# Six VectorE operations instead of eight for each chunk of a float64 to float32 conversion, with the exponent test on ScalarE's absolute value

## The chip, the cores and the metric

The kernel runs on one core of a Trainium2 chip. The metric is the device time of one execution in microseconds; lower is better.

## The reference

Three layers follow each other. Attention takes q, k and v of shape 4 x 8 x 576 x 64, with keys and values averaged over groups of 8 positions. A mixture of 8 experts with matrices of 512 x 1024 and 1024 x 512 works on 2304 tokens, with shares that come from eight rounds of normalising rows and columns. A softplus layer of 512 x 2048 and 2048 x 512 ends the work. The last layer's weights are float64 on the way in, because they are multiplied by a float64 scalar; the kernel gets each number as two 32-bit words.

```python
def _moe_ref(x, w_gate, w1, w2):
    ...
    for e in range(E):
        h = np.maximum(x @ w1[e], 0.0)
        ye = h @ w2[e]
        out += P[:, e:e + 1] * ye
    return out.astype(np.float32)

def _moe2_setup():
    ...
    return {'x': ..., 'w_in': np.random.randn(d_model, d_ff).astype(np.float32) * (1.0 / np.sqrt(d_model)), 'w_out': np.random.randn(d_ff, d_model).astype(np.float32) * (1.0 / np.sqrt(d_ff))}

def _moe2_ref(x, w_in, w_out):
    h = x @ w_in
    g = np.maximum(h, 0.0) + np.log1p(np.exp(-np.abs(h)))
    return (g @ w_out).astype(np.float32)
```

## The kernel before

The 2304 tokens are worked in three parts of 768. Six phases follow each other: the experts for parts 0, 1 and 2, then the softplus layer for parts 1, 2 and 0. Each phase is a row of units, a unit being 256 columns of the hidden layer (32 units for the experts of a part, 8 for the softplus layer). Each unit has a first product (`first`, seven products of half blocks by a fast matrix multiplication scheme, with the sums `u`, `za` and `p` on VectorE) and a second product (`second`, six tiles `py` of 128 tokens, each added into `g` on VectorE). Every operand of TensorE is split into a rounded part (`hi`, written by ScalarE) and a remainder (`lo`, written mostly by GpSimd, L282), and each product is made of three matmuls (L734).

The order of every engine's work is the order in which the program is written. Between the products of `first` and behind the tiles of `second` the main loop calls `hook()`. After the attention and a list of side jobs are done, each hook runs the next step of a generator, `from_float64`, up to its next `yield`. So the conversion of the float64 weights lies between the main operations of the first two expert phases, one VectorE operation per hook. Whatever has not run by the third phase is run there at once.

The conversion has 32 chunks of 128 x 512 numbers. `fetch` (L1163) loads the words of the next chunk into one of two `f64` tiles (shown as `f` in the profile). A chunk then has these steps:

- L1179 and L1181: `da` (in PSUM) gets the exponent and mantissa bits of the upper word shifted by three, and the two sign and top exponent bits
- L1183: `db` gets the 11 exponent bits alone
- L1185: the three top bits of the lower word go into `da`
- L1187: `dt` is `da` as a float, or zero where the exponent is under 897
- L1189: `da` keeps sign and exponent of `dt`
- L1191 and L1193: `dr` is the remaining 29 bits of the lower word, scaled by 2 to the -52 and by `da`
- L1194, on GpSimd: `dt` + `dr`; L1195, on SyncE's queue: the store of `dt` into `v1` or `v2`, and two more hooks' ends

`db` and `dt` have the same tag, `ln`, with two buffers in turn, so every `db` lies in the one and every `dt` in the other. The write of a chunk's `dt` must wait until the store of the chunk before has read its buffer out. `dr` shares the tag `ex`, also with two buffers. GpSimd's queue holds, between these additions, the remainders `w1lo` and `w2lo`, the `sums` of the first weights (L279, L282), and in the second phase the subtractions for `t` that the third phase needs. SyncE's queue issues the stores and the loads of weights (L271, L275, L1163, L345) in the order of the program.

Of the kernel before, what the change touches and what calls it, by code (L numbers as in the profile page):

```python
# [9 lines left out]
F32 = mybir.dt.float32  # L10
F32R = mybir.dt.float32r
U32 = mybir.dt.uint32
AF = mybir.ActivationFunctionType
ALU = mybir.AluOpType
# [5 lines left out]
def attention_moe_softplus_kernel(  # L20
# [12 lines left out]
    nc = tc.nc  # L33
# [10 lines left out]
    P = 128  # L44
# [35 lines left out]
    def bank(name, kind="y", dt=F32):  # L80
        if kind not in banks:
            kind = away[0] or ""
        if kind in halves:
            return banks[kind].tile([P, 2, 512], dt, tag=f"two{kind}", name=name)[:, 0, :]
        return banks[kind].tile([P, 512], dt, tag=f"bank{kind}", name=name)
# [1056 lines left out]
    def widths():  # L1142
        for u in range(NU2):
            o = u * US
            src = w_in[:, 2 * o:2 * (o + US)].rearrange("(c p) (f w) -> p c f w", p=P, w=2)
            for s in range(2):
                yield src[:, 2 * s:2 * s + 2], v1[u][:, 2 * s:2 * s + 2, :]
            src = w_out[o:o + US, :].rearrange("(c p) (d w) -> p c d w", p=P, w=2)
            for s in range(2):
                yield src[:, s:s + 1], v2[u][:, s:s + 1, :]  # L1150

    def from_float64():

        ts, stt = nc.vector.tensor_scalar, nc.vector.scalar_tensor_tensor
        every = list(widths())

        def fetch(i):
            if i < len(every):
                src = every[i][0]
                t = extra["f64"] if i % 2 else tpool.tile([P, 2 * UC * HALF], U32, tag="f64", name="f64", bufs=1)  # L1160
                _, c, f, w = src.shape
                raw_t["f64", i] = t.rearrange("p (c f w) -> p c f w", c=c, w=w)
                nc.sync.dma_start(raw_t["f64", i], src)  # L1163

        fetch(0)
        for _ in range(4):
            yield
        for at, (src, dst) in enumerate(every):
            _, c, f, _ = src.shape
            n = c * f  # L1170
            raw = raw_t.pop(("f64", at))
            fetch(at + 1)
            up = raw[:, :, :, 1].rearrange("p c f -> p (c f)")
            dn = raw[:, :, :, 0].rearrange("p c f -> p (c f)")
            a = bank("da", "c", U32)
            b = tpool.tile([P, n], U32, tag="ln", name="db")
            r = tpool.tile([P, n], U32, tag="ex", name="dr")
            t = tpool.tile([P, n], F32, tag="ln", name="dt")
            ts(a, up, 3, 0x3FFFFFF8, op0=ALU.logical_shift_left, op1=ALU.bitwise_and)  # L1179
            yield  # L1180
            stt(a, up, 0xC0000000, a, op0=ALU.bitwise_and, op1=ALU.bitwise_or)  # L1181
            yield
            ts(b, up, 20, 0x7FF, op0=ALU.logical_shift_right, op1=ALU.bitwise_and)  # L1183
            yield
            stt(a, dn, 29, a, op0=ALU.logical_shift_right, op1=ALU.bitwise_or)  # L1185
            yield
            stt(t, b, 897.0, a.bitcast(F32), op0=ALU.is_ge, op1=ALU.mult)  # L1187
            yield
            ts(a, t.bitcast(U32), 0xFF800000, None, op0=ALU.bitwise_and)  # L1189
            yield  # L1190
            ts(r, dn, 0x1FFFFFFF, None, op0=ALU.bitwise_and)  # L1191
            yield
            stt(r.bitcast(F32), r, 2.0 ** -52, a.bitcast(F32), op0=ALU.mult, op1=ALU.mult)  # L1193
            nc.gpsimd.tensor_tensor(t, t, r.bitcast(F32), op=ALU.add)  # L1194
            nc.sync.dma_start(dst.rearrange("p c f -> p (c f)"), t)  # L1195
            yield
            yield


    conversion = from_float64()  # L1200
    side = []
    slot = [0]
# [176 lines left out]
    tpool = None  # L1379
# [47 lines left out]
    for step, (what, n) in enumerate(todo):  # L1427
# [66 lines left out]
        else:  # L1494
# [53 lines left out]
            if attn[0] is None and "" in banks:  # L1548
                part_banks()
                tpool = pools[0]  # L1550
# [30 lines left out]
```

## Time and profile before

| | us |
|---|---|
| median of 3 runs | 1994.94 |
| lowest and highest | 1991.36 and 1995.46 |
| the profiled execution | 1994.42 |
| its span in the trace | 1992.6 |
| TensorE busy | 1959.6 (98%) |
| VectorE busy | 1423.2 (71%) |
| GpSimd busy | 1387.1 (70%) |
| ScalarE busy | 899.7 (45%) |
| conversion, first to last operation | 362 to 1076 |

The page gives the share of the whole span; an engine can be nearly full in one stretch and half empty in another, so the stretches have to be read by themselves. An idle time in brackets behind an instruction is that of its engine just before it, with what ended it. PE is TensorE, DVE is VectorE, ACT is ScalarE, POOL is GpSimd, SPq is the queue of SyncE.

### The profile page before, as it was taken

The page shows a single profiled execution, that of the slowest core. Times are in us where ns is not written, and L with a number is a line of the kernel's source. Part 1 is how long each engine was busy: PE and PEld are TensorE (multiplying, and loading weights), DVE is VectorE, ACT ScalarE, POOL GpSimd, SP SyncE. Part 2 cuts the span into 40 slices and gives each one's busy share as a digit, 9 for nine tenths or more (in the row PEclk, how much of TensorE's full clock was granted, in tenths as well). Part 3 has the DMA queues.
Part 4 walks back from the last instruction along what each step waited for, and adds up shares of the span by engine and source line. Part 5 has one row for each costly group of instructions (what it writes and reads, how often), then busy time and mean ns, then how long its engine had stood idle before and what let it go on. Part 6 is the DMA issues. An engine that isn't in the chain of part 4 may idle for free. (4 is left out here: it accounts for less than half of the span.)

```text
span 1992.6 us, 29835 instructions
## 1 busy us (share of the span) xinstructions
PE 1959.6 (98%) x10786; PEld 1784.2 (90%) x10786; DVE 1423.2 (71%) x2418; ACT 899.7 (45%) x1710; POOL 1387.1 (70%) x1088
## 2 busy tenths in 40 slices
PE   9899999999999999999999999999999999999999
PEld 7688888899889989889988999999999988888998
DVE  6776576887675898679997667678778657556455
ACT  6545434324434233333333454554455566565543
POOL 6765556766676898856766687788888875656553
PEclk9999999999999999999999999999999999999999
DMA  7342222434344655546565644444545523423421
GB/s 198 106 123 73 67 64 65 158 127 153 136 142 162 226 191 201 183 163 211 174 206 173 213 137 128 150 134 138 175 156 142 173 75 130 152 85 119 150 64 64
DMA packets 183249, 283.43 MB, mean 142 GB/s; under 512 B 31676, under 2 KB 111036, under 8 KB 182844
## 3 DMA queue, kind: packets, MB, share of 16 engines
q1 hardware_dynamic: 173020, 267.75, 42.1%
q10 hardware_dynamic: 10080, 13.77, 1.9%
q8 instruction: 85, 1.39, 0.3%
q14 instruction: 64, 0.52, 0.1%
HBM read 216.23 MB, written 65.24 MB: 141 GB/s over the span
## 5 line engine op out<-in xcount | busy, mean ns | idle before, releaser
L734 PE MATMUL p<-xhi,w1hi 128*128 128x384 f32 x1680 | 570.0, 339 | 11.0 <-DVE p L974 8.7
L734 PE MATMUL p<-xhi,w1lo 128*128 128x384 f32 x1680 | 563.9, 336 | 0.0
L734 PE MATMUL p<-xlo,w1hi 128*128 128x384 f32 x1680 | 563.7, 336 | 0.0
L282 POOL TENSOR_TENSOR w1lo<-w1raw,w1hi 128x512 fp32r<-128x512 f32 x240 | 240.7, 1024 | 361.5 <-ACT w1hi L313 361.5
L734 PE MATMUL py<-w2hi,hhi 128*128 128x512 f32 x1056 | 416.5, 394 | 6.6 <-DVE g L1046 3.3
L734 PE MATMUL py<-w2hi,hlo 128*128 128x512 f32 x1056 | 414.7, 393 | 0.0
L734 PE MATMUL py<-w2lo,hhi 128*128 128x512 f32 x1056 | 414.4, 392 | 0.0
L282 POOL TENSOR_TENSOR w2lo<-w2raw,w2hi 128x1024 fp32r<-128x1024 f32 (+1 forms) x178 | 327.5, 1849 | 61.2 <-ACT w2hi L237 45.4
L734 PEld LDWEIGHTS p<-xhi,w1hi 128*128 128x128 f32 x1680 | 316.2, 188 | 27.7 <-DVE p L974 12.4
L734 PEld LDWEIGHTS p<-xlo,w1hi 128*128 128x128 f32 x1680 | 316.3, 188 | 6.8
L734 PEld LDWEIGHTS p<-xhi,w1lo 128*128 128x128 f32 x1680 | 315.9, 188 | 0.0
L282 POOL TENSOR_TENSOR w1lo<-sums,w1hi 128x1024 fp32r<-128x1024 f32 x120 | 288.8, 2406 | 1.9 <-ACT w1hi L313 1.9
L734 PEld LDWEIGHTS py<-w2hi,hhi 128*128 128x128 f32 x1056 | 198.8, 188 | 51.9 <-DVE g L1046 5.4
L734 PEld LDWEIGHTS py<-w2hi,hlo 128*128 128x128 f32 x1056 | 198.6, 188 | 42.2
L747 ACT ACTIVATE hhi<-p 128x384 fp32r<-128x384 f32 x256 | 121.0, 494 | 255.3 <-PE p L734 222.9
L1061 DVE SCALAR_TENSOR_TENSOR g<-py,prob,g 128x512 f32<-128x512 f32 x282 | 209.6, 745 | 31.1 <-PE py L734 27.4
L734 PEld LDWEIGHTS py<-w2lo,hhi 128*128 128x128 f32 x1056 | 198.7, 188 | 35.7
L978 ACT COPY za<-p 128x384 f32<-128x384 f32 x88 | 42.4, 482 | 329.0 <-PE p L734 325.7
L748 DVE SCALAR_TENSOR_TENSOR hlo<-p,hhi 128x384 fp32r<-128x384 f32 x256 | 140.6, 550 | 21.1 <-ACT hhi L747 21.0
L974 DVE TENSOR_TENSOR za<-p,za 128x384 f32<-128x384 f32 x88 | 48.9, 556 | 123.8 <-PE p L734 123.6
L313 ACT CAST w1hi<-sums 128x1024 fp32r<-128x1024 f32 x120 | 126.2, 1052 | 1.8 <-POOL sums L282 1.8
L734 PE MATMUL py<-hhi,w2lo 128*128 128x384 f32 x360 | 121.7, 338 | 0.9 <-POOL w2lo L282 0.9
(159 smaller groups left out, 3168.3 us busy)
## 6 DMA issues: line engine op xcount, KB each, us to landing
w1raw<-in_moe_w_dram SPq DMA_DIRECT2D x96, 512.0 KB
w2raw<-in_moe_w_dram SPq DMA_DIRECT2D x64, 512.0 KB
sums<-sd SPq DMA_DIRECT2D x48, 512.0 KB
sd<-sums SPq DMA_DIRECT2D x32, 512.0 KB
td<-t SPq DMA_DIRECT2D x64, 256.0 KB
w2raw<-td SPq DMA_DIRECT2D x64, 256.0 KB
xlod<-xl ACTq DMA_DIRECT2D x70, 192.0 KB
xlo<-xlod SPq DMA_DIRECT2D x35, 384.0 KB
```

The costliest lines, as they stand in the source:

```text
L282: nc.gpsimd.tensor_tensor(o, a, b, op=ALU.subtract)
L313: nc.scalar.copy(at(hi), src)
L734: nc.tensor.matmul(ps, lhs[a], rhs[b], start=first and i == 0, stop=last and i == 2, skip_group_check=goes_on,)
L747: nc.scalar.activation(hh, src, AF.Relu)
L748: nc.vector.scalar_tensor_tensor(hl, src, 0.0, hh.bitcast(F32), op0=ALU.max, op1=ALU.subtract)
L974: add = lambda o, x, y: nc.vector.tensor_tensor(o, x, y, op=ALU.add)
L978: nc.scalar.copy(a, ps("a"))
L1061: nc.vector.scalar_tensor_tensor(a, py, prob[:, t, e:e + 1], a, op0=ALU.mult, op1=ALU.add)
```

## The change

The exponent test no longer takes the 11 exponent bits out of the upper word. ScalarE writes the absolute value of the upper word, read as a float32, into `db`; its upper exponent bits and the lower three in the mantissa make the comparison with 1.125 x 2 to the -15 the same test as an exponent of at least 897. The three top bits of the lower word are no longer put into `da`; instead the whole lower word, shifted by one, goes into the remainder `dr`. Six VectorE operations and one ScalarE operation are left for a chunk, and seven hooks instead of nine.

```diff
@@ -1173,25 +1173,22 @@
             up = raw[:, :, :, 1].rearrange("p c f -> p (c f)")
             dn = raw[:, :, :, 0].rearrange("p c f -> p (c f)")
             a = bank("da", "c", U32)
-            b = tpool.tile([P, n], U32, tag="ln", name="db")
-            r = tpool.tile([P, n], U32, tag="ex", name="dr")
+            b = tpool.tile([P, n], F32, tag="ln", name="db")
+            r = tpool.tile([P, n], F32, tag="ex", name="dr")
             t = tpool.tile([P, n], F32, tag="ln", name="dt")
             ts(a, up, 3, 0x3FFFFFF8, op0=ALU.logical_shift_left, op1=ALU.bitwise_and)
+            nc.scalar.activation(b, up.bitcast(F32), AF.Abs)
             yield
             stt(a, up, 0xC0000000, a, op0=ALU.bitwise_and, op1=ALU.bitwise_or)
             yield
-            ts(b, up, 20, 0x7FF, op0=ALU.logical_shift_right, op1=ALU.bitwise_and)
-            yield
-            stt(a, dn, 29, a, op0=ALU.logical_shift_right, op1=ALU.bitwise_or)
-            yield
-            stt(t, b, 897.0, a.bitcast(F32), op0=ALU.is_ge, op1=ALU.mult)
+            stt(t, b, 1.125 * 2.0 ** -15, a.bitcast(F32), op0=ALU.is_ge, op1=ALU.mult)
             yield
             ts(a, t.bitcast(U32), 0xFF800000, None, op0=ALU.bitwise_and)
             yield
-            ts(r, dn, 0x1FFFFFFF, None, op0=ALU.bitwise_and)
+            ts(r.bitcast(U32), dn, 1, None, op0=ALU.logical_shift_right)
             yield
-            stt(r.bitcast(F32), r, 2.0 ** -52, a.bitcast(F32), op0=ALU.mult, op1=ALU.mult)
-            nc.gpsimd.tensor_tensor(t, t, r.bitcast(F32), op=ALU.add)
+            stt(r, r.bitcast(U32), 2.0 ** -51, a.bitcast(F32), op0=ALU.mult, op1=ALU.mult)
+            nc.gpsimd.tensor_tensor(t, t, r, op=ALU.add)
             nc.sync.dma_start(dst.rearrange("p c f -> p (c f)"), t)
             yield
             yield
```

In the changed program `dt` is written by line 1184, `dr` by 1188 and 1190, and GpSimd's addition is line 1191; the work of the other lines is the same. The number behind a tile's name tells one buffer's use from another. On VectorE, in a unit of the second phase, from the accumulation before the first product to the sums behind its fourth, before:

```order
L1061 SCALAR_TENSOR_TENSOR g3_3007<-py_7089,prob_88,g3_3007 128x512
L1181 SCALAR_TENSOR_TENSOR da_7084<-f64_3020,da_7084 128x512
L1061 SCALAR_TENSOR_TENSOR g3_3007<-py_7098,prob_88,g3_3007 128x512
L1183 TENSOR_SCALAR db_7085<-f64_3020 128x512
L974 TENSOR_TENSOR u1_7117<-p6_7127,za_7116 128x384
L1185 SCALAR_TENSOR_TENSOR da_7084<-f64_3020,da_7084 128x512
L1187 SCALAR_TENSOR_TENSOR dt_7087<-db_7085,da_7084 128x512
L1189 TENSOR_SCALAR da_7084<-dt_7087 128x512
L974 TENSOR_TENSOR za_7116<-p6_7127,za_7116 128x384
```

and at the same main operations now:

```order
L1061 SCALAR_TENSOR_TENSOR g3_3007<-py_7114,prob_88,g3_3007 128x512
L1190 SCALAR_TENSOR_TENSOR dr_7036<-dr_7036,da_7034 128x512
L1061 SCALAR_TENSOR_TENSOR g3_3007<-py_7125,prob_88,g3_3007 128x512
L974 TENSOR_TENSOR u1_7143<-p6_7153,za_7142 128x384
L1179 TENSOR_SCALAR da_7162<-f64_7032 128x512
L1182 SCALAR_TENSOR_TENSOR da_7162<-f64_7032,da_7162 128x512
L1184 SCALAR_TENSOR_TENSOR dt_7165<-db_7163,da_7162 128x512
L974 TENSOR_TENSOR za_7142<-p6_7153,za_7142 128x384
```

The end of one chunk (`dr_7036`) and the writing of the next chunk's `dt` now stand within the same two products, where before one chunk had its middle. On GpSimd, in the same unit, before:

```order
L282 TENSOR_TENSOR t_3018<-w2raw_3019,t_3018 128x512
L282 TENSOR_TENSOR t_3018<-t_3018,w2raw_3019 128x512
L279 TENSOR_TENSOR sums_7111<-w1raw_7029 128x256
L282 TENSOR_TENSOR sums_7111<-w1raw_7029 128x256
L282 TENSOR_TENSOR sums_7111<-sums_7111,w1raw_7029 128x256
L282 TENSOR_TENSOR sums_7111<-w1raw_7029,sums_7111 128x256
L1194 TENSOR_TENSOR dt_7087<-dt_7087,dr_7086 128x512
```

and now:

```order
L282 TENSOR_TENSOR w2lo1_124<-w2raw_3019,w2hi1_123 128x1024
L282 TENSOR_TENSOR t_3018<-w2raw_3019,w2raw_125 128x512
L282 TENSOR_TENSOR t_3018<-w2raw_3019,t_3018 128x512
L282 TENSOR_TENSOR t_3018<-t_3018,w2raw_3019 128x512
L1191 TENSOR_TENSOR dt_7037<-dt_7037,dr_7036 128x512
L279 TENSOR_TENSOR sums_7137<-w1raw_7059 128x256
L282 TENSOR_TENSOR sums_7137<-w1raw_7059 128x256
```

The addition of the chunk that ends here stands right behind the subtractions for `t`, ahead of the sums. A later unit of the same phase, on VectorE, now:

```order
L1190 SCALAR_TENSOR_TENSOR dr_9428<-dr_9428,da_9426 128x512
L1061 SCALAR_TENSOR_TENSOR g3_3007<-py_9518,prob_88,g3_3007 128x512
L1061 SCALAR_TENSOR_TENSOR g3_3007<-py_9526,prob_88,g3_3007 128x512
L1179 TENSOR_SCALAR da_9535<-f64_9424 128x512
L1061 SCALAR_TENSOR_TENSOR g3_3007<-py_9541,prob_88,g3_3007 128x512
L1182 SCALAR_TENSOR_TENSOR da_9535<-f64_9424,da_9535 128x512
L1184 SCALAR_TENSOR_TENSOR dt_9538<-db_9536,da_9535 128x512
L974 TENSOR_TENSOR u1_9555<-p6_9565,za_9554 128x384
```

Here `dt` has moved to the place behind the last accumulation of the unit and directly ahead of `u`; GpSimd's addition of `dr_9428` stands behind the subtractions for `t` as in the unit above.

## Rows read from the trace of the kernel before

**Rows 1.** The page, busy us of each engine, share of the span, instructions.
```profile
PE 1959.6 (98%) x10786; PEld 1784.2 (90%) x10786; DVE 1423.2 (71%) x2418; ACT 899.7 (45%) x1710; POOL 1387.1 (70%) x1088
```

**Rows 2.** Stretches of the conversion: length, busy us by engine, granted clock, DMA share, GB/s.
```profile
361.00:465.00 104.00, 103.75 (x524) 93.81 (x522) 91.04 (x151) 30.26 (x57) 70.78 (x58) 1.00 0.49 157
...
648.00:775.00 127.00, 126.62 (x638) 114.44 (x637) 117.04 (x194) 39.00 (x72) 111.49 (x91) 1.00 0.60 202
880.00:1077.00 197.00, 195.47 (x981) 176.26 (x980) 180.51 (x310) 60.71 (x112) 135.63 (x91) 1.00 0.58 191
361.00:1077.00 716.00, 712.69 (x3567) 641.94 (x3566) 578.76 (x984) 249.34 (x466) 513.26 (x395) 1.00 0.52 174
```

**Rows 3.** Groups by line and form: count, busy us, mean ns, idle before.
```profile
L237 ACT CAST w2hi<-w2raw 128x512 fp32r<-128x512 f32 x90 | 53.1, 621 | 40.2 <-DMA w2raw<-td 37.2 <-POOL w2lo L282 3.0
...
L1194 POOL TENSOR_TENSOR dt<-dt,dr 128x512 f32<-128x512 f32 x32 | 41.7, 1303 | 69.4 <-DVE dr L1193 54.9 <-issue 9.5 <-PE p L734 4.8
...
L1183 DVE TENSOR_SCALAR db<-f 128x512 uint32<-128x512 uint32 x32 | 26.9, 841 | 0.0
...
L1185 DVE SCALAR_TENSOR_TENSOR da<-f,da 128x512 uint32<-128x512 uint32 x32 | 21.9, 683 | 0.0
L1187 DVE SCALAR_TENSOR_TENSOR dt<-db,da 128x512 f32<-128x512 uint32 x32 | 21.8, 682 | 7.2 <-DMA v<-dt 4.7 <-POOL sums L282 1.4
...
L1191 DVE TENSOR_SCALAR dr<-f 128x512 uint32<-128x512 uint32 x32 | 19.8, 618 | 0.0
```

**Rows 4.** Timeline near 1058 us: start, length, engine, operation [idle before, releaser].
```profile
1054.52 1.48 POOL L1194 TENSOR_TENSOR dt<-dt,dr 128x512 f32<-128x512 f32 x1
...
1055.23 0.68 DVE L1185 SCALAR_TENSOR_TENSOR da<-f,da 128x512 uint32<-128x512 uint32 x1
...
1056.03 0.33 SPq L1195 DMA_DIRECT2D v<-dt  x1
...
1058.46 0.69 DVE L1187 SCALAR_TENSOR_TENSOR dt<-db,da 128x512 f32<-128x512 uint32 x1 [2.55 <-DMA v<-dt]
...
1058.90 0.39 PE L734 MATMUL py<-w2lo,hhi 128*128 128x512 f32 x1
...
1059.13 0.40 PE L734 MATMUL py<-w2hi,hlo 128*128 128x512 f32 x1
...
1060.37 1.03 DVE L974 TENSOR_TENSOR p<-p,za 128x384 f32<-128x384 f32 x2
1060.99 0.44 PE L734 MATMUL p<-xhi,w1hi 128*128 128x384 f32 x1 [1.46 <-DVE p L974]
```

**Rows 5.** Timeline near 745 us, the same columns.
```profile
745.11 0.69 DVE L1187 SCALAR_TENSOR_TENSOR dt<-db,da 128x512 f32<-128x512 uint32 x1 [1.38 <-POOL sums L282]
...
746.13 0.40 PE L734 MATMUL py<-w2hi,hlo 128*128 128x512 f32 x1
...
746.91 0.44 PE L734 MATMUL p<-xhi,w1hi 128*128 128x384 f32 x1 [0.38 <-DVE p L974]
```

**Rows 6.** Timeline of VectorE and GpSimd, 676 to 682 us.
```profile
676.75 0.75 DVE L1061 SCALAR_TENSOR_TENSOR g<-py,prob,g 128x512 f32<-128x512 f32 x1
...
678.92 0.56 DVE L974 TENSOR_TENSOR u<-p,za 128x384 f32<-128x384 f32 x1 [0.85 <-PE p L734]
...
680.55 1.29 POOL L282 TENSOR_TENSOR t<-t,w2raw 128x512 f32<-128x512 f32 x1
...
681.97 0.56 DVE L974 TENSOR_TENSOR za<-p,za 128x384 f32<-128x384 f32 x1 [0.38 <-PE p L734]
```

**Rows 7.** Timeline of VectorE and GpSimd, 927 to 932 us.
```profile
927.94 0.74 DVE L1061 SCALAR_TENSOR_TENSOR g<-py,prob,g 128x512 f32<-128x512 f32 x1
...
929.99 0.55 DVE L974 TENSOR_TENSOR u<-p,za 128x384 f32<-128x384 f32 x1
930.50 1.28 POOL L282 TENSOR_TENSOR t<-t,w2raw 128x512 f32<-128x512 f32 x1
```

## The prediction

> **What bounds the kernel now.** I read the busy times of the page first, then the stretch tables, then the groups by line, then the timeline at the two places where the conversion already held TensorE up. TensorE is busy for 1959.6 of 1992.6 us [rows 1]. The change lies wholly in the conversion, whose 32 chunks run between 361 and 1077 us. There TensorE is busy for 712.69 of 716 us at a granted clock of 1.00 [rows 2]: only 3.31 us of idle can be won in the whole stretch. VectorE is the next engine: in the three dense parts it is busy for 91.04 of 104, 117.04 of 127 and 180.51 of 197 us, 88 to 92%, and GpSimd for 111.49 of 127 us in the middle one. ScalarE has room (249.34 of 716 us). So the removed 49 us of VectorE work are not time of the kernel; they count only through the moments at which TensorE waited for VectorE.
>
> Two such moments are shown. At 1055.91 VectorE had nothing left before it could write `dt`, because the store of the previous chunk's `dt` (two buffers of one tag, shared with `db`, so `dt` always lands in the same one) was still on its way: GpSimd's addition ran from 1054.52, the store was issued at 1056.03, and `dt` started at 1058.46, 2.43 us after the issue. VectorE sat idle for 2.55 us. The three additions behind it came late, and TensorE's next product began 1.86 us after the matmul before, where 0.23 us is usual: 1.63 us lost [rows 4]. At 745.11 the same wait of 1.38 us cost 0.55 us, 0.78 less 0.23 [rows 5]. So at this place a wait of VectorE costs TensorE the wait less about 0.9 us (0.92 and 0.83). That is the rule I carry through.
>
> **The change, part by part.** *Removed:* two operations of a chunk, 32 times 841 ns and 32 times 683 ns: 48.8 us of VectorE [rows 3]. On the path this is nothing but the two waits above, since the operations beside them leave TensorE busy. *Kept:* the logical shift of the lower word has the form of the masking before it, 618 ns [rows 3]; the other kept operations stay at 0.68 to 0.69 us. *Added:* 32 times Abs on ScalarE. The trace has none from a strided source; the nearest row is the 128x512 cast at 621 ns [rows 3]. It might cost as little as nothing to anyone, and as much as 32 times 0.62 = 20 us if all of it lay in front of what TensorE waits for; ScalarE's idle share of two thirds [rows 2] and two hook steps between Abs and its reader cover it, so I take 0. A wait is added with it: ScalarE now waits for the landing of `f64`, with copies and relus queued behind. VectorE's first operation of the chunk waits for the same landing anyway; I take 0 here and put a late landing into the upper rival.
>
> *Moved:* this is the part that decides. Every step of the conversion takes one hook of the main program. A chunk had nine hooks, now seven. Between the last step of one chunk (`dr`, after which GpSimd adds and SyncE stores) and the writing of `dt` in the next there were six hooks, now four. The chain that must fit between them keeps its length: 1.30 us on GpSimd [rows 3], 0.03 us to the issue of the store and 2.4 us from there to the landing [rows 4], 3.7 to 3.8 us in all, plus whatever GpSimd has still to do when `dr` is ready.
>
> I placed the order of the change between the main operations at the times that these have in the trace. First place: `dr` of the earlier chunk now stands ahead of the accumulation at 676.75, `dt` of the next behind `u` (ends 679.48) and two operations of 0.69, thus at 680.9. But GpSimd's addition is queued behind the three subtractions for `t`, the last of which ends at 681.84 [rows 6]. Addition until 683.1, store issued at 683.2, landed at 685.6: VectorE waits about 4.8 us. It lost nothing there before. Second place: `dt` would start at 929.3, one operation of 0.69 us after the accumulation that ends at 928.68; GpSimd is free at 931.78 [rows 7], so the landing is at 935.5: a wait of 6.2 us, and the `u` that TensorE needs next is right behind it.
>
> The same working at all 32 chunks gives 15 waits, in the order of the chunks 1.3, 1.3, 2.0, 1.6, 4.8, 2.1, 2.3, 2.4, 3.1, 3.4, 3.7, 6.2, 1.9, 1.0 and 1.3 us: 38.4 us in all. Four of them (1.3, 1.3, 1.9, 1.3) arise with an idle GpSimd, purely because four hooks are shorter than 3.8 us; in the others GpSimd is still at other work for 1.2 to 6.3 us when `dr` is ready. Less 0.9 us for each, TensorE would lose 38.4 - 13.5 = 24.9 us. That is the upper end. The lower end has the two large waits alone, 3.9 + 5.3 = 9.2 us: GpSimd's lateness at the other places would shrink once TensorE, and with it all that TensorE paces, has been held up, since GpSimd's queue goes on meanwhile. I take half of the remaining 15.7 us, because a GpSimd that is 88% busy in that part wins room, but not at once: 9.2 + 7.8 = 17 us. What is late next, behind each of these stalls, is VectorE's `u` and `p` additions and the accumulations; they catch up only by what VectorE has free.
>
> *Won back:* the two stalls of 1.63 and 0.55 us. The conversion ends 64 hook steps of 288 earlier, so the one at 1058 finds no conversion any more. Loads behind the stores on SyncE's queue keep their order and gain the time by which a store comes earlier or lose it with a late addition; none of them was waited for at the two places, so they count as 0.
>
> **Sum.** The profiled execution took 1994.42 us, 0.5 below the median of 1994.94. 1994.4 - 2.2 + 17 = **2009 us**. The case's own range: 1994.4 - 2.2 + 9.2 = 2001 to 1994.4 - 2.2 + 24.9 = 2017.
>
> The trace shows 2.43 us from the issue of the 256 KB store to the operation that waited for it [rows 4]. The Trainium skill (DMA: Bandwidth & Descriptors, the section on the chain of events and its two cost components) gives a fixed cost of about 2.0 us and a part for the bytes at 436 GB/s, fitted for transfers issued by GpSimd: an estimate of 2.6 us. By it every wait would be 0.2 us longer, 3 us over the 15, and the sum 2012; the trace's own duration stands. By that rule the 2.4 us are mostly not a matter of bandwidth, so they would not shrink where the DMA engines are less busy.
>
> **The rivals.**
> *A: GpSimd is no longer late, nothing is lost, and a little is won (not slower).* VectorE has six operations instead of eight, so `dr` comes sooner in each chunk, GpSimd adds before it starts on its longer runs, and the store lands in time. Only the four waits with an idle GpSimd and the remainders of the others stay, 2.3 us after the cover: 1994.4 - 2.2 + 2.3 = 1994.5; with nothing left at all the bound is the idle time of the stretch, 1994.4 - 3.3 = 1991.1. It decides if GpSimd reaches the addition before `t`'s subtractions at the two places. For it: GpSimd idles for tens of us in front of this addition, 54.9 us waiting for `dr` [rows 3]. Against it: the order fixes the addition behind `t`, whatever VectorE does.
> *B: the upper end and more.* GpSimd stays as late as in the trace, and the fetch of `f64`, which stands behind the late stores on SyncE, lands late for ScalarE's Abs as well: 2017 to some 2024 (two places of 3 to 4 us on top). For it: the fetch is issued after the store in one queue. Against it: TensorE is already held at those places.
> *C: only the two large waits, partly covered:* 1999 to 2001.
> *D: the change doesn't do what it says*, ScalarE being late with Abs so that VectorE waits for it in every chunk. The order sets Abs two hooks ahead of its reader, and ScalarE is idle for two thirds of the stretch; 1 in 100, counted in B.
>
> **Chances.** 0.2%, 4 us, is about what a measurement of this kernel can tell from no change. The forecast (2001 to 2017) 0.70, B 0.07, C 0.06, A and what lies between it and C 0.17; of the last 0.03 lies more than 4 us below the median, which the 3.3 us of idle time hardly allow. Slower 0.83, same 0.14, faster 0.03. The range leaves out the lower part of A and the outer part of B: 1997 to 2020.
>
> **What would show it.** Right: VectorE's wait for the store ahead of `dt` grows from the 4.7 + 1.4 us of [rows 3] to 25 us or more; TensorE's waits for `u`, `p` or the accumulations grow by 10 us or more, all before about 1000 us; the conversion ends near 1000 us; VectorE's busy time falls by some 49 us and ScalarE's grows by some 20. Wrong: if VectorE's waits grow as said and TensorE stays at its idle time, the cover of 0.9 us is mis-sized; if the waits stay under 10 us, GpSimd's lateness was mis-placed; if ScalarE's waits for `f64` hold TensorE, the part taken as 0 was wrong.

## The result, and the profile after

The changed kernel takes 2012.10 us (median; 2009.05 to 2018.19), the kernel before 1992.11 us in the runs beside it: a ratio of 1.0098, 95% interval 1.0084 to 1.0111. That is 20.0 us more, although VectorE has less to do. The profiled execution of the changed kernel is the longest of its runs, 2018.19 us; so I compared the start of the n-th matmul in the two executions (both have 10786, in the same order) to see where its 23.5 us of longer span arise. 3.5 us are there when the conversion begins, from the attention, whose program is the same (3.1 us at 600). Then:

| stretch, in times of before | TensorE falls behind by (us) |
|---|---|
| 600 to 800 | +9.5 |
| 800 to 900 | 0.0 |
| 900 to 1000 | +15.9 |
| 1000 to 1100 | -2.3 |
| 1100 to the end | -2.6 |

The last line lies in phases that the change doesn't touch, so some 3 us either way belong to the two executions and not to the change. The page of the changed kernel, busy us of each engine:

```profile
PE 1971.8 (98%) x10786; PEld 1789.5 (89%) x10786; DVE 1384.0 (69%) x2354; ACT 917.7 (46%) x1742; POOL 1382.8 (69%) x1088
```

Against [rows 1] VectorE is busy for 39.2 us less, ScalarE for 18.0 us more. The stretches, in the columns of [rows 2]:

```profile
361.00:465.00 104.00, 104.00 (x522) 93.71 (x521) 89.85 (x150) 36.38 (x67) 76.32 (x62) 1.00 0.45 153
...
648.00:775.00 127.00, 122.61 (x603) 107.28 (x602) 102.39 (x175) 45.43 (x84) 106.88 (x90) 1.00 0.61 204
...
361.00:1077.00 716.00, 699.00 (x3449) 623.83 (x3448) 528.40 (x902) 263.20 (x489) 498.70 (x388) 0.99 0.50 170
```

The idle time of TensorE in the stretch of the conversion has grown from 3.31 to 17.00 us. The first dense part, 361 to 465, loses nothing: its waits are short. The groups of the conversion by line and form:

```profile
L1191 POOL TENSOR_TENSOR dt<-dt,dr 128x512 f32<-128x512 f32 x32 | 41.4, 1294 | 71.5 <-DVE dr L1190 50.1 <-issue 15.2 <-DMA f<-in_moe_w_in_dram 6.1
...
L1179 DVE TENSOR_SCALAR da<-f 128x512 uint32<-128x512 uint32 x32 | 21.9, 684 | 6.9 <-DMA f<-in_moe_w_in_dram 3.5 <-DMA f<-in_moe_w_out_dram 3.3
L1184 DVE SCALAR_TENSOR_TENSOR dt<-db,da 128x512 f32<-128x512 f32 x32 | 21.9, 684 | 26.7 <-DMA v<-dt 19.1 <-POOL sums L282 3.3 <-POOL w1lo L282 3.1
...
L1180 ACT ACTIVATE db<-f 128x512 f32<-128x512 f32 x32 | 21.6, 676 | 50.7 <-DMA f<-in_moe_w_out_dram 27.8 <-DMA f<-in_moe_w_in_dram 23.0
```

The mean of each operation is what it was in [rows 3] (`dr` of L1188 624 ns, forecast 618; but it takes 410 to 2146 ns, the median is 418). What changed is the idle time of VectorE ahead of `dt`: 19.1 + 3.3 + 3.1 = 25.5 us for the store of the chunk before (where GpSimd is named it was the store too: `dt` starts 2.1 to 2.4 us after its issue), where it was 4.7 + 1.4. A second, smaller wait has grown: VectorE's first operation and ScalarE's Abs wait for the load of `f64`. What TensorE waited for, 340 to 1110 us (us in total, times, longest), first before, then after:

```profile
PE p L734 <- DVE p L974: 1.8, 2, 1.5
PE py L734 <- DVE g L1061: 1.4, 5, 0.3
```

```profile
PE py L734 <- DVE g L1061: 9.7, 12, 4.2
PE p L734 <- DVE u L974: 4.8, 2, 3.4
PE p L734 <- DVE p L974: 2.4, 4, 1.3
```

The largest waits can be read one by one. The first of the two places that the prediction named lies near 687 us now (timeline of the changed kernel, the columns of [rows 4]):

```profile
681.28 0.67 DVE L1190 SCALAR_TENSOR_TENSOR dr<-dr,da 128x512 f32<-128x512 uint32 x1
...
683.18 1.31 POOL L1191 TENSOR_TENSOR dt<-dt,dr 128x512 f32<-128x512 f32 x1
...
684.00 0.70 DVE L1182 SCALAR_TENSOR_TENSOR da<-f,da 128x512 uint32<-128x512 uint32 x1
...
684.51 0.34 SPq L1192 DMA_DIRECT2D v<-dt  x1
...
686.75 0.69 DVE L1184 SCALAR_TENSOR_TENSOR dt<-db,da 128x512 f32<-128x512 f32 x1 [2.05 <-DMA v<-dt]
...
688.55 0.44 PE L734 MATMUL p<-xhi,w1hi 128*128 128x384 f32 x1 [0.31 <-DVE p L974]
```

The chain is the one forecast, addition, issue, 2.24 us to `dt`, but the wait is 2.05 us instead of 4.8. Against the matmuls of before, TensorE loses about 0.5 us here. The second place, forecast at 929, is at 949:

```profile
941.19 0.67 DVE L1190 SCALAR_TENSOR_TENSOR dr<-dr,da 128x512 f32<-128x512 uint32 x1
...
944.19 1.29 POOL L282 TENSOR_TENSOR t<-t,w2raw 128x512 f32<-128x512 f32 x1
...
944.36 0.68 DVE L1182 SCALAR_TENSOR_TENSOR da<-f,da 128x512 uint32<-128x512 uint32 x1
...
945.44 1.28 POOL L1191 TENSOR_TENSOR dt<-dt,dr 128x512 f32<-128x512 f32 x1
946.75 0.33 SPq L1192 DMA_DIRECT2D v<-dt  x1
...
949.21 0.69 DVE L1184 SCALAR_TENSOR_TENSOR dt<-db,da 128x512 f32<-128x512 f32 x1 [4.18 <-DMA v<-dt]
949.82 0.55 DVE L974 TENSOR_TENSOR u<-p,za 128x384 f32<-128x384 f32 x1
...
950.42 0.69 PE L734 MATMUL p<-xhi,w1hi 128*128 128x384 f32 x1 [3.38 <-DVE u L974]
```

VectorE is done with `da` at 945.04 and can't write `dt` until 949.21, and TensorE stands behind the `u` that follows. GpSimd's subtractions for `t` end at 945.48, 0.4 us after VectorE is ready, where the prediction had 2.5 us (931.78 against 929.3). The wait is 4.18 us instead of 6.2.

The longest stall of TensorE, near 994, was not forecast. The chain of the work that ended there (start, us, what):

```profile
985.99 1.30 POOL dt L1191
...
987.30 6.57 DMA v<-dt
...
994.00 0.69 DVE dt L1184
...
995.16 0.67 DVE g L1061
...
995.87 1.22 PE py L734 x2
```

The store was issued 3.3 us before VectorE was ready for `dt` (990.6), time enough at 2.4 us; but it took 6.57 us instead of 2.33 (946.75 to 949.08, for the store read above). The queue of SyncE shows what was issued around it:

```profile
983.67 0.46 SPq L1163 DMA_DIRECT2D f<-in_moe_w_out_dram  x1
984.17 2.33 SPq L345 DMA_DIRECT2D td<-t  x4
987.30 0.32 SPq L1192 DMA_DIRECT2D v<-dt  x1
987.73 1.08 SPq L1163 DMA_DIRECT2D f<-in_moe_w_out_dram  x1
```

A load of 512 KB and four stores of `t` of 256 KB were issued in the 3.6 us ahead of it, another load 0.4 us behind it. At 946.75 a load and four stores of `t` were issued too, but behind the store, and it landed in 2.33 us. In the kernel before, two stores with four stores of `t` in the 3.8 us ahead of them (1025.11 and 962.51) had their `dt` 4.2 us after their issue. So in these rows a late store is one that has other transfers ahead of it on the queue. TensorE's start at 995.87 is 4.57 us after the one before it.

Two waits of TensorE are of another kind. The one of 1.4 us for `u` (702.34) comes after VectorE had waited for the load, and the one of 1.73 us at 778.62 after `dr` had taken 2.15 us instead of 0.42, while GpSimd was at a subtraction of 2.40 us from 774.76 on:

```profile
697.90 0.69 DVE L1179 TENSOR_SCALAR da<-f 128x512 uint32<-128x512 uint32 x1 [2.34 <-DMA f<-in_moe_w_in_dram]
...
775.30 2.15 DVE L1188 TENSOR_SCALAR dr<-f 128x512 uint32<-128x512 uint32 x1
...
778.62 0.50 PE L734 MATMUL py<-w2hi,hhi 128*128 128x512 f32 x1 [1.73 <-DVE g L1061]
```

### The profile page after: what moved, and what is told of

Read it like the earlier page. It is cut to its first block, busy times and chain, and to the rows that moved or that the text cites. A ratio compares the mean times of both kernels' runs of the same rounds, so it can differ in the third digit from the quotient of the medians.

```text
span 2016.1 us, 29740 instructions
## 1 busy us (share of the span) xinstructions
PE 1971.8 (98%) x10786; PEld 1789.5 (89%) x10786; DVE 1384.0 (69%) x2354; ACT 917.7 (46%) x1742; POOL 1382.8 (69%) x1088
## 4 chain that ended last, share of the span: by engine, by line
PE 81%; POOL 6%; DVE 5%; ACT 3%; DMA 3%; issue 2%; ACTq 0%; SPq 0%; DVEq 0%; POOLq 0%
PE py L734 40%; PE p L734 37%; POOL w1lo L282 2%; POOL w2lo L282 1%; DMA v<-dt 1%; POOL t L282 1%; ACT w1hi L313 1%; PE s L466 1%; DMA xlod<-xl 1%; DVE p L974 1%; PE px L511 1%; POOL dt L1191 1%; PE pa L501 1%; DMA f<-in_moe_w_in_dram 1%; DVE za L974 0%
```

## The experiments

The theory after the result: the loss is the wait of `dt` for the store of the chunk before, which has too few hooks to land in. The rivals: the late load of `f64`; the spacing itself, that is VectorE's operations packed more closely in front of those that TensorE needs; and GpSimd's lateness. All ratios are to the kernel before in runs beside them (median 1992.8 to 1993.8 us). Differences between two experiments are taken from their medians; by the ratios most are within 1 us of that, and where they are not both are given.

**Two buffers for `dt`** (e1). `db` moves to the other tag, so `dt` gets both buffers of its own.

```diff
-            b = tpool.tile([P, n], F32, tag="ln", name="db")
+            b = tpool.tile([P, n], F32, tag="ex", name="db")
```

> The changed kernel with db moved to the other tag, so that dt alternates between two buffers and never waits for the store of the chunk just before; seven hooks, six VectorE operations and ScalarE's Abs stay. Store theory (the four hooks between the end of a chunk and the next dt are shorter than GpSimd's queue, addition and store): the waits ahead of dt vanish, and of the 20 us lost some 15 or more come back, 1992 to 1998 us. Fetch theory (ScalarE's Abs and VectorE's first step wait for the f64 words, and the copies and relus behind Abs hold TensorE): little comes back, 2006 to 2012 us.

Measured: 1999.86 us, ratio 1.0034 (1.0022 to 1.0046). The value lies between the two theories. No wait of `dt` for a store is left, and 12.2 us are gone; 6.5 us over the kernel before remain, and what waits now is the load (waits of ScalarE: total, times, longest; VectorE's first operation has another 12.6 us in five):

```profile
ACT db L1180 <- DMA f<-in_moe_w_out_dram: 23.6, 3, 9.0
ACT db L1180 <- DMA f<-in_moe_w_in_dram: 22.6, 6, 9.6
```

**Nine hooks again** (e2). The six operations, with two empty steps ahead of `dt`.

```diff
             stt(a, up, 0xC0000000, a, op0=ALU.bitwise_and, op1=ALU.bitwise_or)
             yield
+            yield
+            yield
             stt(t, b, 1.125 * 2.0 ** -15, a.bitcast(F32), op0=ALU.is_ge, op1=ALU.mult)
```

> The changed kernel with two empty hooks put in where the two removed operations stood: six operations and Abs, but nine hooks for a chunk. Spacing theory: both the store and the fetch find their old distance, 1990 to 1994 us, the same as before or up to 3 us better, since the idle time of TensorE in that stretch was 3.3 us. ScalarE theory (Abs in ScalarE's queue is itself what costs): still above 2000 us.

Measured: 1991.49 us, ratio 0.9987 (0.9976 to 0.9997). The whole loss is gone with all six operations and ScalarE's Abs in place. So what costs is the number of hooks, not Abs and not the new arithmetic. The waits are not all gone: `dt` still waits 11.4 us for stores, in eight places, but TensorE's named waits are 3.7 us, against 3.2 in the kernel before. This alone doesn't tell why: a chunk of nine hooks gives the store, the load and VectorE more room alike.

**Seven hooks with the eight old operations** (e3). This one is made from the kernel before; two of the steps do two operations each.

```diff
             ts(a, up, 3, 0x3FFFFFF8, op0=ALU.logical_shift_left, op1=ALU.bitwise_and)
+            ts(b, up, 20, 0x7FF, op0=ALU.logical_shift_right, op1=ALU.bitwise_and)
             yield
             stt(a, up, 0xC0000000, a, op0=ALU.bitwise_and, op1=ALU.bitwise_or)
-            yield
-            ts(b, up, 20, 0x7FF, op0=ALU.logical_shift_right, op1=ALU.bitwise_and)
-            yield
             stt(a, dn, 29, a, op0=ALU.logical_shift_right, op1=ALU.bitwise_or)
             yield
```

> The kernel before, with all eight VectorE operations and no Abs, but packed into seven hooks (the exponent bits beside the first step, the three lower bits beside the second). Spacing theory: as slow as the change or slower, since VectorE has more to do in each hook: 2008 to 2025 us. ScalarE theory: as fast as before, 1990 to 1996 us.

Measured: 2025.36 us, ratio 1.0159 (1.0142 to 1.0176), slower than the change by 13 us. TensorE's idle time in the stretch is 716 - 691.43 = 24.57 us. `dt` waits only 10.8 us for stores here, against 25.5 in the change, and TensorE waits 11.9 us for `u`, in ten places, against 4.8 in two. So this loss is not the change's over again: VectorE's operations packed in front of those that TensorE needs cost as well, once there are eight of them.

```profile
361.00:1077.00 716.00, 691.43 (x3402) 614.64 (x3401) 563.04 (x955) 241.02 (x449) 498.29 (x384) 0.99 0.51 169
```

**The absolute value on VectorE** (e4), as a mask, in the hook of the first operation.

```diff
-            nc.scalar.activation(b, up.bitcast(F32), AF.Abs)
+            ts(b.bitcast(U32), up, 0x7FFFFFFF, None, op0=ALU.bitwise_and)
```

> The changed kernel with the absolute value taken by VectorE (a bit mask) beside the first step, so that ScalarE has no part in the conversion; seven hooks. Store theory: the waits ahead of dt stay, 2006 to 2016 us. Fetch theory: ScalarE's copies and relus no longer stand behind a wait for the f64 words, and most of the loss goes, 1992 to 2000 us.

Measured: 2021.04 us, ratio 1.0139 (1.0119 to 1.0159). Both theories missed: taking ScalarE out of it costs 8.9 us. `dt` waits 22.8 us for stores here and VectorE's first operation 5.4 us for the load, a little less than in the change (25.5 and 6.8), but TensorE's named waits are 21.4 us instead of 16.9. So ScalarE's wait for the load is not what makes the loss. That the seventh VectorE operation (415 to 2206 ns) makes the 8.9 us is what is left; no run takes it apart.

**Early loads** (e5). Each `f64` buffer is loaded again right behind its last read, ahead of the store, instead of at the start of the next chunk.

```diff
         fetch(0)
+        fetch(1)
...
-            fetch(at + 1)
...
             ts(r.bitcast(U32), dn, 1, None, op0=ALU.logical_shift_right)
+            fetch(at + 2)
             yield
```

> The changed kernel with the f64 words of chunk i+2 fetched right behind the last read of chunk i's, ahead of the store of chunk i on SyncE's queue; dt still waits for the store of the chunk before. After the two dt buffers alone took 13 of the 20 us back, the store theory says that the store waits stay here: 2003 to 2009 us, the fetch's own share of 6 to 7 us gone. If fetch and store waits hide behind each other at the same places, nothing goes: 2010 to 2013 us. If the fetch were the root of both, 1990 to 1996 us.

Measured: 2013.43 us, ratio 1.0103 (1.0087 to 1.0118), no gain. No operation waits for the load any more, but `dt` waits longer for the stores:

```profile
DVE dt L1184 <- DMA v<-dt: 23.3, 12, 5.0
```

With three more waits that the profile puts down to ScalarE and GpSimd (Abs had ended 4.7 and 6.8 us before the two of ScalarE) it is 30.2 us, against 25.5 in the change. The load now stands ahead of the store on the queue, and at four of the 14 places the store takes clearly longer than at the same place of the change, from issue to `dt`: 3.38 instead of 2.21 us, 2.94 instead of 2.14, 4.01 instead of 2.51, 4.29 instead of 2.79. So the time that the load gave back went into the stores.

**Two buffers and early loads** (e6), both edits together.

> The changed kernel with both: dt in two buffers of its own and the early fetch; seven hooks stay. Two-wait theory (store and fetch together are the whole loss): 1989 to 1994 us, level with before or up to 3 us better. If something else in the seven hooks costs (VectorE's density, GpSimd behind dr, ScalarE's Abs in its queue), it stays above 1996 us.

Measured: 1988.73 us, ratio 0.9984 (0.9974 to 0.9993). TensorE is busy for all but 2.26 us of the stretch:

```profile
361.00:1077.00 716.00, 713.74 (x3578) 644.31 (x3577) 543.81 (x923) 268.36 (x500) 511.64 (x397) 1.00 0.52 174
```

So with both waits gone the whole loss is gone, although six operations and Abs still stand in seven hooks: the closer spacing of six costs nothing by itself. The two waits are not additive: without the store's wait 12.2 us go (e1), without the load's nothing (e5), without both 23.4. They lie in front of the same operations, and by e5 the one transfer also delays the other.

**The addition on VectorE** (e7), in the kernel of the change, to take GpSimd's lateness out of the chain.

```diff
-            nc.gpsimd.tensor_tensor(t, t, r, op=ALU.add)
+            nc.vector.tensor_tensor(t, t, r, op=ALU.add)
```

> The changed kernel with the last addition on VectorE instead of GpSimd, so that the store is issued without GpSimd's queue in the chain; one dt buffer, late fetch and seven hooks stay. If GpSimd's lateness is what makes most of the store waits (29 of my 38 us), the waits ahead of dt fall to a few us and the fetch, no longer behind late stores on SyncE's queue, comes earlier too: 1994 to 2002 us, with 32 times some 0.6 us more on VectorE. If the short distance alone makes them, it stays at 2008 to 2016 us.

Measured: 2010.18 us, ratio 1.0084 (1.0069 to 1.0099): the waits of the first theory with the time of the second. The waits for the store fell to 6.7 us, so most of them did come with GpSimd's part in the chain, but the time stayed. e11 below tells the likely reason.

**Everything** (e8): nine hooks, two buffers and early loads.

> The changed kernel with two dt buffers, the early fetch and nine hooks. With all waits gone nothing but the idle time of TensorE in the stretch can be won: 1988 to 1992 us, no different from seven hooks with both repairs by more than 2 us. If the conversion's six operations spread over nine hooks collide less with the sums of the second phase, it is the faster of the two.

Measured: 1988.31 us, ratio 0.9980 (0.9972 to 0.9988): no difference from e6 that can be told. Where the buffers are free, the hooks don't matter.

**The kernel before with two buffers and early loads** (e9). The two edits of e6 on the eight operations and nine hooks.

> The kernel before, eight VectorE operations and nine hooks, with the two buffer edits of the best version: dt in two buffers in turn, each load of f64 issued right behind the last read of its buffer. Theory 1, the buffers give all that was gained over the kernel before and the six operations nothing: 1987 to 1990 us, as with the six operations (1988.7 and 1988.3). Theory 2, the kernel before loses only 3.3 us in the stretch of the conversion, of which the buffers take the two waits of dt (2.2 us), and the rest comes from the shorter VectorE work: 1990.5 to 1993. No wait of dt for a store is left in either.

Measured: 1988.10 us, ratio 0.9972 (0.9959 to 0.9985). TensorE's idle time in the stretch is 1.40 us:

```profile
361.00:1077.00 716.00, 714.60 (x3581) 644.83 (x3580) 583.04 (x988) 251.91 (x471) 516.80 (x397) 1.00 0.52 174
```

The first theory holds. The gain over the kernel before comes from the buffers and the loads; six operations instead of eight add nothing to it that can be told. e6, e8 and e9 beat both kernels, the one before by 4 to 6 us (3 to 6 by the ratios) and the change by 23 to 24 us.

**The absolute value on VectorE, with free buffers** (e10): the edits of e4 and e6.

> Two buffers of dt and early loads, with the absolute value as a mask on VectorE instead of ScalarE, so seven VectorE operations in seven hooks. Theory 1, what it cost before the buffers were freed (2021.0 against 2012.1) was later stores only: with the buffers free it is 1988 to 1991. Theory 2, it is VectorE's load in seven hooks, two operations in one hook in front of what TensorE waits for: 1994 to 2003, with waits of TensorE for u, p and g of 6 us or more.

Measured: 1991.39 us, ratio 0.9989 (0.9977 to 1.0001), 0.4 us above the first theory and under the second. The seventh operation cost 8.9 us in e4 and costs 2.7 us here (1 us by the ratios), within what the two intervals leave open; TensorE's named waits are no longer than in e6. So the load of VectorE counted mainly where it came on top of the waits.

**The addition on VectorE, with free buffers** (e11): the edits of e7 and e6.

> Two buffers of dt and early loads, with the last addition of a chunk on VectorE instead of GpSimd. Theory 1, the addition on VectorE is what kept the run with the addition there at 2010.2 although the waits for the store had fallen to 6.7 us: 1998 to 2008, with waits of TensorE for g and u of 8 us or more. Theory 2, it was the waits for the store and for the load that were left: 1988 to 1993.

Measured: 2003.18 us, ratio 1.0037 (1.0026 to 1.0048): 14.5 us over e6 with nothing else changed (some 10.6 by the ratios, 1.0037 against 0.9984), and no wait of VectorE for a store or a load. TensorE waits 5.5 us for `g` and 3.3 us for `u`. The addition itself is the cost; its row gives the shortest, median and longest duration in ns, and the timeline its longest one:

```profile
L1192 DVE TENSOR_TENSOR dt<-dt,dr x32: 691/946/2736, 366.6 to 992.8; 128x512 f32<-128x512 f32 x32
```

```profile
685.88 2.38 POOL L282 TENSOR_TENSOR w1lo<-sums,w1hi 128x1024 fp32r<-128x1024 f32 x1
...
686.07 2.74 DVE L1192 TENSOR_TENSOR dt<-dt,dr 128x512 f32<-128x512 f32 x1
...
688.22 2.81 POOL L282 TENSOR_TENSOR w2lo<-w2raw,w2hi 128x1024 fp32r<-128x1024 f32 x1
...
689.99 0.50 PE L734 MATMUL py<-w2hi,hhi 128*128 128x512 f32 x1 [2.17 <-DVE g L1061]
```

The addition starts 0.19 us behind an operation of GpSimd and ends at 688.81, 0.55 us after that has ended; TensorE then misses `g`. So e7 missed because it traded the wait for the store against this one. That settles e7's time only by analogy: its own addition reached 2742 ns as well.

## Why the prediction was right, and where it was not

**The bound and the direction: right.** VectorE lost 48.6 us of operations (178.3 us in eight groups of before, 129.7 us in six; the page's 39.2 us counts the overlap of neighbouring operations once) and TensorE gained nothing from it. e9 against e6 shows it without the waits: no difference that can be told.

**The place: right.** "Between the last step of one chunk [...] and the writing of `dt` in the next there were six hooks, now four": e2 gives two hooks back and the loss is gone; e1 gives `dt` a second buffer and 12.2 us go. VectorE's wait ahead of `dt` is 25.5 us (said: 25 or more), TensorE's named waits grew from 3.2 to 16.9 us (said: 10 or more), and the last stall ends at 996 us (said: before about 1000). The conversion ends at 1012 instead of near 1000, since the stalls delay the conversion too.

**The waits' size: too large by half.** The term "15 waits [...] 38.4 us in all" measured 25.5 us. The number of waits came out, 15; their length did not. The step that failed is that in most of them "GpSimd is still at other work for 1.2 to 6.3 us when `dr` is ready", placed at the times of before. At the two places read above GpSimd was less late against VectorE: 0.4 us instead of 2.5 at 949, and at 687 it had begun the addition (683.18) before VectorE was ready for `dt` (684.70), so the wait was 2.05 instead of 4.8 us. By then TensorE had been held up, and VectorE with it, while GpSimd's queue went on. The prediction said so for its lower end and then took half; for the large waits it should have applied it as well.

**What a wait costs TensorE: about right for the stores, but other costs were left out.** "The wait less about 0.9 us" with the measured 25.5 us and 15 waits gives 25.5 - 13.5 = 12 us. In the comparison of the matmuls, TensorE's seven stalls right behind a wait for a store add up to 11.7 us. Single waits differ: 2.05 us cost 0.5, 4.18 us cost 3.54 (the 3.72 us between two starts less the usual 0.18), and 3.39 us cost 4.34, since VectorE had already waited 2.07 us for the load just ahead. But from 600 to 1000 us TensorE lost 9.5 + 15.9 = 25.4. Of the rest the trace names three parts, all of which the prediction had at nothing:

- The late load, as rival B had it: 1.6 us at 702.34, and 0.66 us at 759.87, where ScalarE's `hhi` stood behind an Abs that had waited 8.47 us for it. The prediction's own sign for this was "if ScalarE's waits for `f64` hold TensorE, the part taken as 0 was wrong". The experiments give it more weight: 11.1 us lie between e1 and e6, once the store is out of the way.
- `dr`, stretched to 2.15 us beside GpSimd: 1.9 us at 778.62, behind a wait of 1.65 us for a store.
- The clock, which fell behind the two longest stalls (below): 4.7 us.

Some 5 us in steps of 0.7 us and less are not put down to anything here.

So that the forecast came near the result is in part luck. One term was too large, other costs were missing, and the half that was taken between the two ends made up for it. The base was luck too: 2009 was 14.8 us over the 1994.4 known then, and the measured loss is 20.0 us over a kernel before that now has a median of 1992.11. Of the 2.2 us won back, the stall of [rows 4] came as said (TensorE regains 1.62 us where it was); the one of [rows 5] did not, since `dt` waits for a store there too (752.42), and 0.2 us are regained.

**Abs on ScalarE at nothing: right.** 676 ns each instead of 621, 21.6 us in all. With free buffers the kernel with Abs takes no longer than the one without, as far as can be told (e6, e9). What was not nothing is the wait for the load that came with it, as above. Rival D needed VectorE to wait for Abs in every chunk; no wait of `dt` names Abs. VectorE's `u` additions have 9.2 us of idle time put down to Abs, but in e6 it is 8.4 us and TensorE loses nothing by it.

**The landing.** The trace's 2.4 us held at nearly all places: 2.24 us from the issue to `dt` at 684.51, 2.33 to the landing at 946.75, and 2.1 to 2.8 us to `dt` wherever it waited, but for one place. That is the store at 987.30 with 6.57 us, which had a load and four stores issued shortly ahead of it. The prediction had no term for that, and this is the wait in front of the longest stall. The Trainium skill (DMA: Bandwidth & Descriptors, the two cost components) gives an estimate of 2.6 us for such a store, by a fit for transfers issued by GpSimd; 2.24 and 2.33 us are shorter than that, 6.57 is far longer.

**The rivals.** A (GpSimd no longer late, nothing lost) is refuted as a whole, though GpSimd was indeed less late than forecast. B's late load came, but not its time: the median lies under 2017. C (only the two large waits) is out: 9.5 us were lost before 800, where the large wait cost 0.5.

## What to carry to other kernels

An operation removed from an engine that is not the bound gives no time by itself; look at what its slot was good for. Here the slots of two removed operations were the time in which a single-buffered result went to memory, and removing the work removed the distance. Before shortening such a chain, give the result a second buffer and issue the next load as soon as its buffer is read: that was worth 6 us without the change (e9) and 23 us with it (e6). The early load alone gave nothing (e5): where two waits lie in front of the same operation, mending one may show nothing, and a load that is issued ahead of a store on one queue can delay the store.

## What the runs showed that I had not expected

After the two longest stalls of TensorE its clock was lower. The stretches around them in the changed kernel (the granted clock is the third number from the right):

```profile
947.00:951.00 4.00, 0.62 (x3) 0.58 (x3) 1.79 (x4) 0.00 (x0) 0.00 (x0) 0.79 0.83 204
951.00:957.00 6.00, 6.00 (x21) 5.53 (x20) 4.50 (x9) 3.01 (x6) 2.54 (x3) 0.57 0.83 298
957.00:965.00 8.00, 8.00 (x38) 6.79 (x37) 7.13 (x13) 2.02 (x4) 6.71 (x5) 1.00 0.58 202
...
991.00:996.40 5.40, 1.22 (x5) 0.73 (x4) 2.40 (x5) 2.83 (x6) 5.40 (x4) 0.75 0.78 277
996.40:1001.00 4.60, 4.60 (x13) 3.58 (x12) 4.17 (x8) 0.41 (x1) 2.31 (x2) 0.55 0.62 212
1001.00:1010.00 9.00, 9.00 (x50) 8.49 (x49) 7.49 (x13) 2.33 (x6) 1.29 (x1) 1.00 0.09 33
```

After the stall of 3.72 us the granted clock was 0.57 for 6 us, after the one of 4.57 us 0.55 for 4.6 us: mostly the lower of the two levels, 1.2 GHz instead of 2.4. Matmuls of 384 columns then start 0.32 us apart instead of 0.18:

```profile
944.10 0.33 PE L734 MATMUL p<-xhi,w1lo 128*128 128x384 f32 x1
944.28 0.33 PE L734 MATMUL p<-xhi,w1hi 128*128 128x384 f32 x1
...
951.23 0.52 PE L734 MATMUL p<-xhi,w1lo 128*128 128x384 f32 x1
951.55 0.52 PE L734 MATMUL p<-xhi,w1hi 128*128 128x384 f32 x1
```

By the granted clock this costs 6.00 x (1 - 0.57) + 4.60 x (1 - 0.55) = 2.6 + 2.1 = 4.7 us on top of the stalls, and the matmuls of before agree: TensorE falls behind by 6.3 and 6.5 us at the two places, of which the stalls themselves are 3.54 and 4.34. The stall of 1.86 us in [rows 4] had no such cost: the granted clock of before is 1.00 in the 5 us after it. So has the changed kernel in the 5 us after 778.62.

The other surprise is the addition on VectorE, 691 ns at its shortest and 2736 ns beside GpSimd in e11. The Trainium skill (SBUF — State Buffer, the section on the two separate sides) has it that an operation of VectorE with two inputs in SBUF and one of GpSimd that reads SBUF exclude each other for their whole length. The rows at 686 us agree: the addition ends only after GpSimd's operation has, and GpSimd's next one, `w2lo`, takes 2.81 us instead of the 2.40 of the others of its form.
